# Fused attention and expert layer on one core: a pair's product with v issued behind the third tile of scores instead of the second

## The chip, the cores and the metric

The kernel runs on one core of one Trainium2 chip. The metric is device time in microseconds (us) of one execution; where several runs are compared, their median. PE is TensorE's matmul side and PEld its weight loads, DVE is VectorE, ACT is ScalarE, POOL is GpSimd, and SP is SyncE, which issues the DMAs of this kernel from one queue (SPq).

## The reference, cut to what matters

Two layers follow each other. The first is causal attention with a decay (4 batches, 8 heads, 576 positions, head size 64), the second a sum over 4 experts on the 2304 rows of its result (width 512, inner width 1024):

```python
scores = scale * np.matmul(q, k.transpose(0, 1, 3, 2))
scores = np.where(causal, -1000000000.0, scores + decay)
scores = scores - np.max(scores, axis=-1, keepdims=True)
attn = np.exp(scores)
attn = attn / (np.sum(attn, axis=-1, keepdims=True) + 1e-09)
x = np.matmul(attn, v)            # heads side by side: (2304, 512)
...
for e in range(4):
    h = np.maximum(x @ w1[e], 0.0)
    out += p[:, e:e + 1] * (h @ w2[e])
```

## The kernel before, in words

Attention is cut into 32 jobs. A job is a batch, a pair of heads and a half of the query rows: the first half is rows 0 to 255, the second half rows 256 to 575 against all 576 keys. All first halves come before all second halves (table JOBS, line 43). The change concerns the 16 jobs of the second half, called pairs here; `s1_0_1_1_4_0`, say, is scores of batch 1, head pair 0, half 1, head 1 of the pair, row tile 4, first piece. The first head of a pair is called even here, the second odd.

A head of the second half takes these steps:

- **Preparation.** ACT rounds q and k to a high part (`hi`, line 568), and POOL forms the rest (lines 569, 577, 583).
- **Scores.** For each of three row tiles (2, 3 and 4) `qk_tile` (line 661) has PE form the scores (line 623) in one of four PSUM banks of the pool `ps_a` (tile 4 is cut into two pieces of 288 columns, in two banks). DVE adds the mask and takes the minimum of the negated row (line 637), and ACT takes the exponential with the row sum (line 652).
- **Reciprocal.** DVE forms it from the row sums (`recip16`, lines 680 and 683).
- **Turning.** `turn16` (line 699) splits the scaled probabilities into two float16 parts, `z` high on ACT (line 721) and `z` low on DVE (line 722), in four pieces, and turns them with three DMA transposes on SP's queue (line 731) into a buffer `pt`, of which there are three for all heads.
- **Product.** `av_pair` (line 811) multiplies both heads' `pt` with v in 28 matmuls (line 823) that alternate between the two heads, into a bank of `ps_a`. `out16` (line 874) copies the result with ACT (line 877) into the expert layer's input.

The experts run at the same time on the rows that are finished: steps of a first product (`l1`, line 1019), a gate on ACT and DVE (`gh`, line 1033, and `gl`, line 1034), a second product (`l2`, line 1053) and a sum on DVE (`acc`, line 1080). Their weights are split in three places of ACT, DVE and POOL (lines 980 to 986). PE has both kinds of work in one stream, and the text calls a wait of PE for `gl` or `acc` a wait for the experts' DVE work.

What sets the order around the change: `head_steps(n)` (line 893) writes down the steps of head n as a list with costs: `qs` holds the three score tiles (584, 712 and 776), the reciprocal and the three turns. Into it goes the product of the pair that ended two heads before (cost 1000), with `out16` and the marks `ready`, after which the rows of a chunk count as finished. This is done only where head n is odd, so each pair's product stands among the score tiles of the next pair's odd head. `pace` (line 1566) hands these steps out between the expert steps in proportion to their costs, and a scheduler of the tile framework then orders each engine's instructions by the dependences. After the last pair the list of scores is empty, so the product of the last pair is not moved among tiles. When the attention is done, the inputs of four more chunks are scaled and combined (lines 261, 1170 to 1172), and a second stage of the experts (line 1291) takes over from about 575 us on.

Of the kernel before, what the change touches and what calls it, by code (L numbers as in the profile page):

```python
# [79 lines left out]
def fused(ctx: ExitStack, tc: tile.TileContext, qk, v, f, probs, w, out):  # L80
# [812 lines left out]
    def head_steps(n):  # L893

        st = []
        if FIRST < n < len(heads) and heads[n][1] == 0:
            st.append((0, heads[n][0].prep_v))
        if n + 1 < len(heads):
            j, hh = heads[n + 1]
            st.append((0, lambda j=j, hh=hh: j.prep(hh)))  # L900
        if n + 2 < len(heads):
            j, hh = heads[n + 2]
            st.append((0, lambda j=j, hh=hh: j.far(hh)))
            st.append((0, lambda j=j, hh=hh: j.load(hh)))
        qs, ts, us = [], [], []
        if n < len(heads):
            j, hh = heads[n]
            for t in j.its:
                qs.append((TOK0[t] + 328, lambda j=j, hh=hh, t=t: j.qk_tile(hh, t)))
            if j.half:  # L910
                qs.append((0, lambda j=j, hh=hh: j.recip16(hh)))
                for t in j.its:
                    qs.append((0, lambda j=j, hh=hh, t=t: j.turn16(hh, t)))
            elif hh == 1:
                qs.append((0, j.recip))
        if n - 2 >= FIRST and heads[n - 2][1] == 1 and heads[n - 2][0].half:
            j = heads[n - 2][0]
            qs[2:2] = [(1000, j.av_pair), (0, j.out16)] + ready(n - 2)
        if n - 2 >= FIRST and heads[n - 2][0].half == 0:
            j, hh = heads[n - 2]  # L920
            late_ = [(200, lambda j=j, hh=hh: j.av(hh))]
            if hh == 1:
                late_ += [(0, j.fin)] + ready(n - 2)
            qs[1:1] = late_
        if FIRST < n <= len(heads):
            j, hh = heads[n - 1]
            for gi in range(len(j.blocks())):
                ts.append((500, lambda j=j, hh=hh, gi=gi: j.tr(hh, gi)))
        if n + 1 < len(heads):
            j, hh = heads[n + 1]  # L930
            us.append((0, lambda j=j, hh=hh: j.begin(hh)))
        for k in range(max(len(qs), len(ts))):
            st += ts[k : k + 1] + qs[k : k + 1]
        return st + us
# [577 lines left out]
    def ready(n):  # L1512
        return [(0, c) for c in sorted(done_at) if done_at[c] == n]
# [3 lines left out]
    for n in range(FIRST, len(heads) + 2):  # L1517
        for cost_, f_ in head_steps(n):
            if type(f_) is int:
                if f_ < LAST[0]:  # L1520
                    asteps.extend(turn(f_))
                need[f_] = len(asteps)
            else:
                asteps.append((cost_, f_))
# [103 lines left out]
    j = heads[FIRST][0]  # L1628
# [162 lines left out]
```

## Time and profile before

| | before |
|---|---|
| median of 3 runs | 910.04 us (909.53 to 910.26) |
| the profiled execution | 913.29 us |
| span of its profile | 911.5 us |
| PE busy | 876.0 us (96%) |
| DVE busy | 712.5 us (78%) |
| ACT busy | 568.8 us (62%) |
| POOL busy | 521.7 us (57%) |

The span is what the profile covers of the profiled execution: 1.79 us of its time lie outside. The profiled execution took 3.25 us (0.36%) more than the median of the runs. Times in rows are counted from the start of the span. The second halves of the attention lie between about 208 and 574 us.

### The profile page before, as it was taken

Reading aid. Unit: us, or ns where it says so; the run is one execution under the profiler, and the core shown is the slowest. Engines: PE = TensorE matmul, PEld = TensorE weight load, DVE = VectorE, ACT = ScalarE, POOL = GpSimd, SP = SyncE. Lnnn points to the kernel's source line nnn. Section 1 sums busy time; section 2 is a strip of 40 time slices with the busy share of each in tenths; the row PEclk is TensorE's granted clock in tenths of the full one; section 3 lists DMA queues with packets and bytes.
Section 4 is the critical chain, followed back from the end, with each engine's and each line's share of the span. In section 5 each row is a group of like instructions: output and inputs, shape, how many; then the busy total and the mean of one; then the engine's idle time right before and its main releaser. Section 6 shows DMA issues by size and latency. Waiting matters only on the chain. (4 is left out here: it accounts for less than half of the span.)

```text
span 911.5 us, 16657 instructions
## 1 busy us (share of the span) xinstructions
PE 876.0 (96%) x5783; PEld 617.8 (68%) x5783; DVE 712.5 (78%) x1464; ACT 568.8 (62%) x1137; POOL 521.7 (57%) x522
## 2 busy tenths in 40 slices
PE   3899999999998999999999999989999999999998
PEld 2789898998876666666766666644456654666547
DVE  5768887877999878899888886766688847787487
ACT  5768876657776667677776775645565445553350
POOL 4656556665465454356552772885778627886160
PEclk9999999999999999999999999999999999999999
DMA  7348763665789969979997998834322424232003
GB/s 271 126 151 288 249 232 124 187 195 167 243 203 234 261 175 241 241 211 208 269 289 174 249 244 182 296 126 138 125 79 95 140 70 139 71 112 74 24 1 94
DMA packets 147508, 159.45 MB, mean 175 GB/s; under 512 B 86148, under 2 KB 107328, under 8 KB 147424
## 3 DMA queue, kind: packets, MB, share of 16 engines
q1 hardware_dynamic: 147424, 158.39, 61.1%
q8 instruction: 45, 0.74, 0.3%
q14 instruction: 39, 0.32, 0.1%
HBM read 117.30 MB, written 21.65 MB: 152 GB/s over the span
## 5 line engine op out<-in xcount | busy, mean ns | idle before, releaser
L1019 PE MATMUL l<-y,w 128*128 128x256 f16 x1248 | 154.1, 274 | 0.0
L652 ACT ACTIVATE p<-p,nm 128x576 f32<-128x576 f32 (+3 forms) x160 | 95.7, 599 | 74.2 <-DVE nm L637 61.2
L1019 PEld LDWEIGHTS <-w 128*128 128x128 f16 x1248 | 117.8, 98 | 30.8 <-issue 7.3
L1053 PE MATMUL l<-w,gh 128*128 128x512 f16 x408 | 122.0, 380 | 1.9 <-DVE acc L1080 1.8
L569 POOL CAST q<-raw 64x320 fp32r<-64x320 f32 (+1 forms) x56 | 27.6, 494 | 145.6 <-PE s L623 119.6
L722 DVE SCALAR_TENSOR_TENSOR z<-p,rs,z 128x384 f16<-128x384 f32 (+3 forms) x128 | 82.8, 673 | 13.2 <-ACT z L721 11.9
L1080 DVE SCALAR_TENSOR_TENSOR acc<-y,scg,acc 128x256 f32<-128x256 f32 (+1 forms) x164 | 80.9, 516 | 12.1 <-PE y L1291 11.7
L577 POOL TENSOR_TENSOR kl<-raw,hi 64x576 fp32r<-64x576 f32 (+1 forms) x56 | 68.0, 1214 | 38.7 <-ACT hi L568 36.7
L623 PE MATMUL s<-hi 128*128 128x384 f32 (+1 forms) x192 | 75.8, 399 | 11.4 <-DVE hi L583 8.8
L1291 PE MATMUL m<-rh,bs 128*128 128x512 f16 x256 | 86.4, 379 | 0.0
L637 DVE CUSTOM_DVE_ANT_0 p<-s,mask 128x288 f32<-128x288 f32 (+2 forms) x160 | 74.7, 475 | 13.4 <-PE s L623 12.7
L1217 POOL TENSOR_TENSOR bs<-wt,bs 128x512 f16<-128x512 f32 x32 | 40.5, 1270 | 66.5 <-ACT bs L1216 66.3
L1053 PE MATMUL l<-w,gl 128*128 128x512 f16 x204 | 77.2, 379 | 0.7 <-DVE gl L1034 0.7
L721 ACT ACTIVATE z<-p,rs 128x384 f16<-128x384 f32 (+3 forms) x128 | 69.4, 589 | 5.7 <-DVE rs L683 2.7
L1019 PE MATMUL l<-xh,wh 128*128 128x256 f32 x224 | 65.7, 295 | 1.0 <-ACT xh L864 1.0
L1019 PE MATMUL l<-xh,wl 128*128 128x256 f32 x224 | 64.9, 292 | 1.4 <-POOL wl L962 1.3
L1034 DVE SCALAR_TENSOR_TENSOR gl<-l,gh 128x512 f16<-128x512 f32 (+1 forms) x80 | 54.8, 685 | 14.5 <-ACT gh L1033 13.9
L1291 PE MATMUL m<-rh,bw 128*128 128x512 f16 x191 | 64.4, 379 | 1.4 <-ACT r L1337 1.4
L623 PE MATMUL s<-kl,q 66*128 66x384 f32 (+1 forms) x192 | 62.7, 331 | 3.2 <-DMA kl<-nc 3.2
L1019 PE MATMUL l<-xl,wh 128*128 128x256 f32 x224 | 65.3, 291 | 0.0
L1033 ACT ACTIVATE gh<-l 128x512 f16<-128x512 f32 (+1 forms) x80 | 47.1, 589 | 26.8 <-PE l L1019 26.2
L1291 PEld LDWEIGHTS <-bs 128*128 128x128 f16 x384 | 37.5, 98 | 38.4
(385 smaller groups left out, 2343.9 us busy)
## 6 DMA issues: line engine op xcount, KB each, us to landing
wr<-in_w SPq DMA_DIRECT2D x90, 512.0 KB
pk<-in_w SPq DMA_DIRECT2D x64, 256.0 KB
wd<-w SPq DMA_DIRECT2D x32, 512.0 KB
raw<-in_qk SPq DMA_DIRECT2D x32, 448.0 KB
bw<-wd SPq DMA_DIRECT2D x32, 256.0 KB
bv<-wd SPq DMA_DIRECT2D x32, 256.0 KB
raw<-in_qk SPq DMA_DIRECT2D x24, 256.0 KB
vp<-in_v SPq DMA_DIRECT2D x10, 512.0 KB
```

The lines of the kernel that those rows point to most:

```text
L577: eng.tensor_tensor(out=kl[:64, :wk], in0=r[:64, ko : ko + wk], in1=hi[:64, ko : ko + wk].bitcast(F32), op=ALU.subtract,)
L623: nc.tensor.matmul(out=ps[:, at : at + z - a], lhsT=lhsT, rhs=rhs, start=(m == 0), stop=(m == 1),)
L637: nc.vector.tensor_tensor_reduce(out=pt[:, a:z], in0=ps, in1=mask[:, m0 + a : m0 + z], scale=-0.125, scalar=BIG if n == 0 else nm[:, col : ...
L652: nc.scalar.activation(out=pt[:, :w_], in_=pt[:, :w_], func=AF.Exp, scale=-1.0, bias=self.nmax[hh][:, c : c + 1], accum_out=self.ssum[:, h ...
L721: nc.scalar.activation(out=o[:, 0], in_=x, func=AF.Copy, scale=sc)
L722: nc.vector.scalar_tensor_tensor(out=o[:, 1], in0=x, scalar=sc, in1=o[:, 0], op0=ALU.mult, op1=ALU.subtract)
L1019: i = nc.tensor.matmul(out=self.l1p[:, fi, :], lhsT=lhsT, rhs=rhs[:, k, :], start=(k == 0 and m == 0), stop=(k == 3 and m == 2),)
L1033: self.first = nc.scalar.activation(out=self.gh, in_=self.l1p, func=AF.Relu)
L1034: self.last = nc.vector.scalar_tensor_tensor(out=self.gl, in0=self.l1p, scalar=0.0, in1=self.gh.bitcast(F32) if wide else self.gh, op0=ALU ...
L1053: matmul(out=l2[tt], lhsT=lhsT, rhs=rhs, start=(self.ps == 0 and fi == 0 and m == 0), stop=(self.ps == 1 and fi == 1 and m == 2),)
L1080: nc.vector.scalar_tensor_tensor(out=acc[c][:, tt, d0:d1], in0=ps, scalar=sc, in1=acc[c][:, tt, d0:d1], op0=ALU.mult, op1=ALU.add,)
L1291: line.append(nc.tensor.matmul(**args))
```

## The change

One line of `head_steps`: the product, its copy and the marks are put into the list at index 3, so behind the score tiles 2, 3 and 4 and ahead of the reciprocal and the turns; before, they stood at index 2, between tiles 3 and 4.

```diff
@@ head_steps(n)
         if n - 2 >= FIRST and heads[n - 2][1] == 1 and heads[n - 2][0].half:
             j = heads[n - 2][0]
-            qs[2:2] = [(1000, j.av_pair), (0, j.out16)] + ready(n - 2)
+            qs[3:3] = [(1000, j.av_pair), (0, j.out16)] + ready(n - 2)
```

It acts on 15 of the 16 pairs. Since the costs keep their places but for this one swap, `pace` hands some steps out earlier or later than before, and the scheduler orders the engines anew. Three places show it.

PE, batch 0: the scores of the odd head of pair 2 (`s0_2_1_1`, tiles 2, 3 and 4) and the product of pair 1 (`o0_1_1`), which is due among them, then the first rows of pair 2's own product (`o0_2_1`). Before:

```order
L623 MATMUL s0_2_1_1_2_0_3643<-hi0_2_1_1_3501 128x384
...
L623 MATMUL s0_2_1_1_3_0_3674<-hi0_2_1_1_3501 128x512
...
L823 MATMUL o0_1_1_3700<-pt0_1_1_0_3310,v20_1_1_3207 64x320
...
L623 MATMUL s0_2_1_1_4_0_3756<-hi0_2_1_1_3501 128x288
...
L623 MATMUL s0_2_1_1_4_1_3759<-hi0_2_1_1_3501 128x288
...
L823 MATMUL o0_1_1_3700<-pt0_1_1_1_3480,v20_1_1_3207 64x320
...
L823 MATMUL o0_2_1_3999<-pt0_2_1_0_3602,v20_2_1_3498 64x320
...
L823 MATMUL o0_2_1_3999<-pt0_2_1_1_3767,v20_2_1_3498 64x320
```

With the change:

```order
L623 MATMUL s0_2_1_1_2_0_3627<-hi0_2_1_1_3481 128x384
...
L623 MATMUL s0_2_1_1_3_0_3654<-hi0_2_1_1_3481 128x512
...
L623 MATMUL s0_2_1_1_4_0_3682<-hi0_2_1_1_3481 128x288
...
L623 MATMUL s0_2_1_1_4_1_3685<-hi0_2_1_1_3481 128x288
...
L823 MATMUL o0_1_1_3715<-pt0_1_1_0_3299,v20_1_1_3194 64x320
...
L823 MATMUL o0_1_1_3715<-pt0_1_1_1_3460,v20_1_1_3194 64x320
...
L823 MATMUL o0_2_1_4008<-pt0_2_1_0_3588,v20_2_1_3478 64x320
...
L823 MATMUL o0_2_1_4008<-pt0_2_1_1_3748,v20_2_1_3478 64x320
```

Between this head's last scores and the first row of its own pair's product stand 254 rows of PE's order before and 326 with the change. For the pairs from 3 to 14 it is about 200 before and about 350 with the change; for the last pair 68 and 148.

DVE, the same head: from its last minimum (`p0_2_1_1_4`) to the low parts of its probabilities (`z1`, `z3`). Before (the rows left out are the second weight split, two sums, four minima of the next head, the preparation of v and rows on scales):

```order
L637 ISA p0_2_1_1_4_3616,nm0_2_1_1_3617<-s0_2_1_1_4_1_3759,mask_115,nm0_2_1_1_3617 128x288
L637 ISA nm0_2_1_1_3617 128x1
L1034 SCALAR_TENSOR_TENSOR gl1_0_2_0_3750<-l1_1_0_2_0_3693,gh1_0_2_0_3749 128x512
L285 TENSOR_REDUCE wmax_121<-pk1_14_3634 128x1
L986 SCALAR_TENSOR_TENSOR w36_3815<-wr36_3253,wsc_122,w36_3815 128x512
...
L680 TENSOR_SCALAR ss0_2_1_3496<-ss0_2_1_3496 128x3
...
L683 RECIPROCAL rs0_2_1_3497<-ss0_2_1_3496 128x3
...
L1034 SCALAR_TENSOR_TENSOR gl1_0_2_1_3865<-l1_1_0_2_1_3834,gh1_0_2_1_3864 128x512
...
L722 SCALAR_TENSOR_TENSOR z1_3003<-p0_2_1_1_2_3614,rs0_2_1_3497,z1_3003 128x3x128
```

With the change:

```order
L637 ISA p0_2_1_1_4_3602,nm0_2_1_1_3603<-s0_2_1_1_4_1_3685,mask_115,nm0_2_1_1_3603 128x288
L637 ISA nm0_2_1_1_3603 128x1
L680 TENSOR_SCALAR ss0_2_1_3476<-ss0_2_1_3476 128x3
L683 RECIPROCAL rs0_2_1_3477<-ss0_2_1_3476 128x3
L722 SCALAR_TENSOR_TENSOR z1_2973<-p0_2_1_1_2_3600,rs0_2_1_3477,z1_2973 128x3x128
L722 SCALAR_TENSOR_TENSOR z1_2973<-p0_2_1_1_3_3601,rs0_2_1_3477,z1_2973 128x4x128
L722 SCALAR_TENSOR_TENSOR z3_2975<-p0_2_1_1_4_3602,rs0_2_1_3477,z3_2975 64x4x128
L722 SCALAR_TENSOR_TENSOR z3_2975<-p0_2_1_1_4_3602,rs0_2_1_3477,z3_2975 64x64
L637 ISA p0_3_1_0_2_3760,nm0_3_1_0_3763<-s0_3_1_0_2_0_3799,mask_115 128x384
```

The odd head's low parts now stand right behind its own minima, where two gate subtractions, two weight splits, two sums, four minima and the preparation of v stood between them before.

POOL, the preparation of the even head of pair 1 and the low parts of two expert weights (`wl30`, `wl31`). Before:

```order
L962 TENSOR_TENSOR wl30_2962<-wr30_2374,wh30_2961 128x512 x2
L962 TENSOR_TENSOR wl31_2969<-wr31_2583,wh31_2968 128x512 x2
...
L569 CAST q2_0_116<-raw0_1_1_0_2867 64x320
L577 TENSOR_TENSOR kl0_1_1_0_2865<-raw0_1_1_0_2867,hi0_1_1_0_3022 64x576
L583 TENSOR_TENSOR hi0_1_1_0_3022<-raw0_1_1_0_2867,hi0_1_1_0_3022 64x320
```

With the change:

```order
L569 CAST q2_0_116<-raw0_1_1_0_2860 64x320
L577 TENSOR_TENSOR kl0_1_1_0_2858<-raw0_1_1_0_2860,hi0_1_1_0_2992 64x576
L583 TENSOR_TENSOR hi0_1_1_0_2992<-raw0_1_1_0_2860,hi0_1_1_0_2992 64x320
L962 TENSOR_TENSOR wl30_3002<-wr30_2374,wh30_3001 128x512 x2
L962 TENSOR_TENSOR wl31_3009<-wr31_2583,wh31_3008 128x512 x2
```

The preparation has moved ahead of the two weights' low parts. On SP's queue the transposes of the odd heads have moved ahead of weight loads and stores in the same way (those of pair 6, for one, now stand ahead of the load `wr46` and of the stores `wd10` and `wd11`).

## Rows read from the trace of the kernel before

**Rows 1.** The page, part 1: busy time of each engine over the whole span.

```profile
PE 876.0 (96%) x5783; PEld 617.8 (68%) x5783; DVE 712.5 (78%) x1464; ACT 568.8 (62%) x1137; POOL 521.7 (57%) x522
```

**Rows 2.** Waits of PE, 240 to 640 us: total us, times, longest us.

```profile
PE o L823 <- DMA pt<-z: 5.5, 4, 2.2
PE l L1053 <- DVE acc L1080: 1.8, 3, 1.3
PE l L1053 <- DVE gl L1034: 0.7, 1, 0.7
```

**Rows 3.** Groups of PE, 240 to 640 us: busy, mean ns, idle before and its releaser.

```profile
L823 PE MATMUL o<-pt,v 128*64 128x320 f16 (+2 forms) x448 | 31.2, 281 | 5.6 <-DMA pt<-z 5.5
```

**Rows 4.** Timeline, odd head and product of pair 2: start, duration, work, [idle before, releaser].

```profile
266.57 0.30 PE L623 MATMUL s<-kl,q 66*128 66x288 f32 x1
...
280.27 2.99 DVE L722 SCALAR_TENSOR_TENSOR z<-p,rs,z 128x384 f16<-128x384 f32 x2 [0.25 <-ACT z L721]
282.01 4.25 SPq L731 DMA_TRANSPOSE pt<-z  x3
...
285.24 0.32 PE L823 MATMUL o<-pt,v 128*64 128x320 f16 x1
...
288.07 1.69 PE L823 MATMUL o<-pt,v 128*64 128x320 f16 x27 [2.19 <-DMA pt<-z]
```

**Rows 5.** Timeline, the last pair: its last transpose and its product.

```profile
567.93 1.23 SPq L731 DMA_TRANSPOSE pt<-z  x1
...
571.91 1.72 PE L823 MATMUL o<-pt,v 128*64 128x320 f16 x27
```

**Rows 6.** Windows: busy us of PE, PEld, DVE, ACT, POOL, granted clock, DMA share.

```profile
240.00:270.00 30.00, 29.59 (x222) 22.97 (x222) 27.97 (x57) 23.18 (x47) 14.21 (x14) 1.00 0.79 192
270.00:300.00 30.00, 27.69 (x199) 19.01 (x198) 28.53 (x59) 22.22 (x46) 18.34 (x14) 1.00 1.03 245
300.00:330.00 30.00, 27.79 (x192) 18.92 (x190) 23.30 (x59) 17.57 (x35) 9.42 (x14) 0.94 0.93 244
450.00:480.00 30.00, 29.32 (x207) 19.51 (x205) 25.96 (x57) 22.47 (x45) 15.37 (x15) 1.00 1.08 275
```

**Rows 7.** Timeline, product of pair 3 and expert matmuls; one from before pair 2's product.

```profile
283.83 1.47 PE L1019 MATMUL l<-y,w 128*128 128x256 f16 x12
...
310.56 2.74 PE L823 MATMUL o<-pt,v 128*64 128x320 f16 x27 [2.21 <-DMA pt<-z]
313.24 2.05 PE L1019 MATMUL l<-y,w 128*128 128x256 f16 x12
```

**Rows 8.** Window of one us behind that wait.

```profile
312.00:313.00 1.00, 1.00 (x14) 0.96 (x11) 0.71 (x2) 0.00 (x0) 0.00 (x0) 0.50 0.96 344
```

**Rows 9.** Groups of DVE by shape, 260 to 570 us.

```profile
L722 DVE SCALAR_TENSOR_TENSOR z<-p,rs,z 64x512 f16<-64x512 f32 x29 | 23.6, 814 | 0.9
L722 DVE SCALAR_TENSOR_TENSOR z<-p,rs,z 128x512 f16<-128x512 f32 x29 | 22.3, 770 | 0.0
L722 DVE SCALAR_TENSOR_TENSOR z<-p,rs,z 128x384 f16<-128x384 f32 x28 | 19.6, 701 | 11.3 <-ACT z L721 11.2
L637 DVE CUSTOM_DVE_ANT_0 p<-s,mask 128x512 f32<-128x512 f32 x27 | 18.4, 680 | 0.1
L637 DVE CUSTOM_DVE_ANT_0 p<-s,mask 128x384 f32<-128x384 f32 x27 | 14.8, 546 | 1.0 <-PE s L623 0.8
L722 DVE SCALAR_TENSOR_TENSOR z<-p,rs,z 64x64 f16<-64x64 f32 x29 | 12.5, 430 | 0.1
```

**Rows 10.** Groups of ACT by shape, 220 to 560 us.

```profile
L652 ACT ACTIVATE p<-p,nm 128x576 f32<-128x576 f32 x30 | 23.2, 773 | 29.0 <-DVE nm L637 28.8
L721 ACT ACTIVATE z<-p,rs 128x384 f16<-128x384 f32 x31 | 18.8, 606 | 4.1 <-DVE rs L683 2.7 <-ACT p L652 0.8 <-ACT gh L1033 0.2
```

**Rows 11.** Waits, whole span: POOL's preparation of heads.

```profile
POOL q L569 <- PE s L623: 126.9, 35, 12.5
```

**Rows 12.** Transposes into pt, whole span: min/median/max ns, first and last.

```profile
L731 SPq DMA_TRANSPOSE pt<-z x96: 1198/1258/4662, 221.6 to 567.9; - x96
```

## The prediction

> **What bounds the kernel.** I read the page's busy times first: PE is busy for 876.0 us of the span and DVE for 712.5 [rows 1], so time is won where PE stands idle, or loses its clock, and nothing on another engine counts unless PE waits for it. Then the waits of PE over the second halves of the attention: the largest entry is the product with v waiting for the transposed probabilities, 5.5 us in four waits, the longest 2.2 [rows 2]. The same stretch's group of line 823 has 5.6 us idle over 448 matmuls, that is 16 pairs of 28 [rows 3]. The 0.1 between them is a fifth, very short wait.
>
> Where do these waits come from? In the timeline of pair 2 the odd head's last scores end at 266.87 (266.57 and 0.30). DVE turns to the low parts of its probabilities only at 280.27, 13.4 us later, the three transposes are issued from 282.01 to 286.26, and PE, which had begun the product at 285.24, waits 2.19 us until 288.07 [rows 4]. The last transpose thus needs 1.8 us from the end of its issue until PE goes on. So a pair waits when its odd head's transposes are issued too late, and most of the lateness is not work of that head. It is DVE doing other things between its minima and its low parts. Pair 3 has the same shape with 2.21 us [rows 7].
>
> Its price is more than the gap. [...] PE's work shows it, since the same 27 matmuls take 2.74 us there and 1.69 at pair 2, and twelve expert matmuls 2.05 instead of 1.47 [rows 4, 7].
>
> **The change, part by part.** The product and the third tile change places, so the product itself costs the same. What counts is the distance from the odd head's last scores to its own product.
>
> *The waits for transposes: -5.6 us.* Before, the product of the pair ahead sat in the middle of the odd head and held its third tile back. Now the tile goes first, and 326 rows of PE's order stand where 254 stood at pair 2, some 350 where 200 stood at the pairs behind it. Every second row is a weight load, which runs beside the matmuls, so 70 more rows are 35 matmuls or, at the 1.47 us of twelve [rows 7], 4.3 us more cover, and 150 rows 9.2. The longest wait is 2.21, so both ends of that are enough. On DVE the low parts now stand right behind the head's own minima, which takes several more us off. I take all five waits as gone: 5.6. The ends are 5.6 and, if SP's queue held the transposes back, 0 (rival B).
>
> *The clock: -0.9 us.* Of two nearly equal waits, 2.19 and 2.21, one was followed by the lower clock and one was not [rows 4, 7, 8]. [...] If new waits arise, the clock may fall behind one of these. Ends -1.8 and 0, the middle taken. [...]
>
> *New waits for DVE: +2.0 us.* DVE's total work is the same, but it comes earlier. In 270 to 300 us DVE is busy for 28.53 us, so 1.47 are free, while PE's time in it shrinks by pair 2's 2.19 us [rows 4, 6]: DVE is 0.7 short. Besides, from the gate subtraction of expert step 0_7_0_1, in which the second halves begin, to that of step 1_1_2_0, counting rows in both orders, DVE has nine heads' low parts now against eight, and one minimum of tile 2 and one of tile 3 fewer. A head's low parts are 0.70 + 0.77 + 0.81 + 0.43 = 2.72 us, the two minima 0.55 + 0.68 [rows 9], so 1.5 us more. Together 2.2; I take 2.0, since some of it falls into 300 to 330 us where DVE has 6.7 us free [rows 6]. It should appear as PE waiting for `gl` or `acc`, as it does now for 0.7 and 1.8 us [rows 2]. Ends: 0, if DVE's overlap between instructions hides it, and 5, if two odd heads also hold DVE up as in rival A.
>
> *POOL and SP: 0.* The preparation of heads mostly waits for the scores of an earlier head to free a buffer (126.9 us in 35 waits [rows 11]), so scores that come earlier are not held by it. Two weights' low parts (`wl30`, `wl31`) have fallen behind one preparation, once in the kernel; their cover is the rest of the expert step, and what is lost if it is missing is bounded by that preparation, under the lower end of the DVE term. On SP's queue weight loads now stand behind transposes. An issue takes 1.26 us at the median and 4.66 at most [rows 12], so a load can be up to 14 us later; a load is issued well ahead of its use and three buffers hold loads, so I put it at nothing, and at 2 us for the high end (a wait like the longest above).
>
> *The last pair and the hand-over: 0.* The last pair is not moved, but the steps around it are. Its last transpose is issued by 569.16 and its product runs from 571.91 without a wait, a distance of 2.75 us against the 1.8 it needs [rows 4, 5], so 1 us of reserve. The order has 148 rows instead of 68 between its scores and its product, so the reserve is not smaller. Behind it the inputs of the next chunks are scaled, and PE waits there for `acc`, 1.3 us at the longest [rows 2]. It can close or double: ends -1.3 and +1.3, taken as 0.
>
> Sum: -5.6 - 0.9 + 2.0 = -4.5 us. The profiled execution took 913.29 us, 3.25 above the median of the runs, so 908.8 against it, and **905.5** against the median of 910.04. I assume that the median's runs have the same waits.
>
> **Rivals.**
>
> *A, slower: DVE stands still behind the odd head's own exponential.* The low parts right behind the last minimum have to wait for ACT: the exponential of tile 4 at 0.77 us and the first high part at 0.61 [rows 10], 1.4 us in which DVE, which takes its instructions in order, does nothing. Before, other rows filled this. DVE already idles 11.2 us for high parts over 28 heads [rows 9]. In the five pairs up to 330 us, with DVE at 27.97 and 28.53 of 30 [rows 6], nothing absorbs it: 5 x 1.4 = 7.0, with the 2.0 above 9.0, against 5.6 saved, and the clock lost again at new waits, so +3.4 and 913.4. It decides when DVE's free time in 240 to 300 us (3.5 us now) is less than what the heads there leave idle. For it: the order, which puts nothing between. Against it: DVE need not keep up at once, since a gate subtraction may be some us late before PE wants it (PE waited for `gl` once from 240 to 640 us [rows 2]).
>
> *B, no change: the wait only moves.* Either the transposes land when the DMA engines let them (their share is 1.03 to 1.08 of the windows with waits and transposes reach 4.66 us [rows 6, 12]), or DVE gives back the 5.6 us whole, about 910.0. For it: DVE is nearly full just where the waits are. Against: 450 to 480 us has the highest share, 1.08, and PE was still busy for 29.32 of 30.
>
> *C, half: given back at the hand-over.* All before 574 us happens as forecast, but the experts' rest waits for weights or for the scaled inputs as the attention ends earlier: half of the gain, 907.8. For it: the `acc` wait of 1.3 us shows that PE has little reserve there.
>
> That the change would not do what it says, as `pace` could hand the steps out so that nothing moves, the orders exclude.
>
> **How the numbers follow.** A measurement of this kernel can tell about 0.2%, 1.8 us, from no change. The forecast gets 0.56, C 0.16, B 0.13, A 0.15. The forecast's own ends are 910.04 - 5.6 - 1.8 - 1.3 = 901.3 and 910.04 - 5.6 + 5 + 2 = 911.4, of which most lies below 908.2. Faster: 0.53 of the forecast and 0.12 of C, 0.65. Same: the rest of both (0.07) and B, 0.20. Slower: A, 0.15. The range goes from 901.8 to 911.4, which leaves out the larger part of A and little else; without A and B it would be 902 to 908.5.
>
> **What would show it.** Right: no idle time, or under 0.5 us, at line 823, and over 5 us from the end of an odd head's transposes to its product; a granted clock of 1.00 over 300 to 330 us; new waits of PE for `gl` or `acc` before 330 us that sum to 1 to 4 us. Rival A shows as DVE idle for ACT at lines 680 and 722 in 210 to 330 us with PE waiting for `gl` for over 5 us; B as waits at line 823 of the same size; C as more than 2 us of PE idle in 574 to 620 us. The forecast is wrong if line 823 still waits for over 2 us in sum, or if the PE waits for DVE before 330 us exceed the saved 5.6.

## The result and the profile after

With the change the kernel took **919.04 us** (median of 4 runs, 917.20 to 920.33), against 909.78 (908.41 to 910.26) for the kernel before in the same comparison: a ratio of 1.0095, interval 1.008 to 1.011. It is slower by about 9 us. I had forecast 905.5 with a range of 901.8 to 911.4, so both the sign and the range were wrong. The profiled execution of the changed kernel took 920.33 us (span 918.6).

The page's busy times answer to [rows 1]:

```profile
PE 876.5 (95%) x5783; PEld 615.4 (67%) x5783; DVE 714.6 (78%) x1464; ACT 568.8 (62%) x1137; POOL 523.6 (57%) x522
```

PE is as busy as before, 876.5 us against 876.0, so the time has gone into idle PE. These are the four largest waits of PE from 240 to 640 us (total us, times, longest us), against [rows 2]:

```profile
PE l L1053 <- DVE acc L1080: 4.0, 3, 2.4
PE o L823 <- DMA pt<-z: 3.0, 2, 2.4
PE m L1291 <- ACT r L1337: 2.5, 1, 2.5
PE topx L200 <- DVE xmax L261: 1.1, 1, 1.1
```

The product with v, which waited 5.5 us in four waits, still waits 3.0, and that in two. The long one of the two is in a new place, the last pair. `topx` (PE turning a maximum that DVE has formed) is new in this stretch, and so are, further down the list, two waits for weights (`w`, 0.8 us each); the wait for `r` (the second stage's copy on ACT) has grown from 0.6 us.

The windows (busy us of PE, PEld, DVE, ACT, POOL, granted clock, DMA share) show where; the first two answer to [rows 6]:

```profile
270.00:300.00 30.00, 30.00 (x216) 20.58 (x216) 26.81 (x57) 23.08 (x48) 18.08 (x15) 1.00 1.04 235
300.00:330.00 30.00, 27.90 (x206) 19.06 (x204) 25.88 (x67) 18.37 (x38) 12.51 (x14) 1.00 0.89 230
...
540.00:570.00 30.00, 27.57 (x207) 18.43 (x205) 19.82 (x42) 15.13 (x33) 10.17 (x7) 0.95 0.69 167
570.00:600.00 30.00, 27.79 (x177) 16.88 (x176) 22.50 (x34) 15.88 (x27) 20.34 (x20) 1.00 0.71 246
600.00:630.00 30.00, 25.07 (x120) 12.06 (x119) 14.55 (x20) 12.66 (x21) 15.90 (x18) 0.94 0.48 158
```

The first two went nearly as forecast: no idle PE from 270 to 300 us, and a clock of 1.00 from 300 to 330 instead of 0.94, with 2.1 us of new waits for DVE. The loss is in the last three, where PE is idle for 2.43, 2.21 and 4.93 us and the clock is below full twice (0.95 and 0.94). The same three windows of the kernel before had PE busy for 30.00, 29.61 and 27.78 us at 1.00. So the change loses its time behind 560 us, at the last pair and the hand-over to the next chunks.

PE's timeline there (start, duration, work, idle before and its releaser):

```profile
551.04 0.30 PE L623 MATMUL s<-kl,q 66*128 66x288 f32 x1
...
559.90 0.32 PE L823 MATMUL o<-pt,v 128*64 128x320 f16 x1
...
562.11 1.69 PE L1019 MATMUL l<-y,w 128*128 128x256 f16 x14
566.23 2.67 PE L823 MATMUL o<-pt,v 128*64 128x320 f16 x27 [2.43 <-DMA pt<-z]
568.83 1.92 PE L1019 MATMUL l<-y,w 128*128 128x256 f16 x10
...
585.11 0.39 PE L1019 MATMUL l<-y,w 128*128 128x256 f16 x2 [0.82 <-ACT w L985]
586.28 2.58 PE L1019 MATMUL l<-y,w 128*128 128x256 f16 x22 [0.78 <-DVE w L986]
...
605.19 0.59 PE L1053 MATMUL l<-w,gh 128*128 128x512 f16 x2 [2.43 <-DVE acc L1080]
...
614.53 0.56 PE L1291 MATMUL m<-rh,bs 128*128 128x512 f16 x1 [2.49 <-ACT r L1337]
```

The first row is the last of the scores of the last odd head. Before, the last product ran without a wait [rows 5]. Now it waits 2.43 us for its transposes, and it stands in the middle of one group of 24 gate matmuls of the experts: 14 of them ahead of it, 10 behind. Four more waits follow, of 0.82, 0.78, 2.43 and 2.49 us. With three short ones between 595 and 599 us (0.14, 0.22, 0.24) this is 9.55 us of idle PE; before, the stretch had 0.29, 1.30, 0.44 and 0.59, so 2.62.

The other queues in that stretch show what links the waits (same columns; ACT, SP's queue, DVE and POOL in order of time):

```profile
552.91 3.19 DVE L986 SCALAR_TENSOR_TENSOR w<-wr,wsc,w 128x512 f16<-128x512 f32 x2
...
558.55 2.21 ACT L721 ACTIVATE z<-p,rs 128x384 f16<-128x384 f32 x4 [0.49 <-ACT p L652]
...
559.88 4.29 SPq L731 DMA_TRANSPOSE pt<-z  x3
...
568.94 0.68 ACT L877 ACTIVATE xf<-o,vun 128x64 f32<-128x64 f32 x2 [6.99 <-PE o L823]
568.99 1.27 POOL L1170 TENSOR_TENSOR rx<-xf,xf 128x512 f32<-128x512 f32 x1 [4.92 <-PE o L823]
569.28 2.35 DVE L261 TENSOR_REDUCE xmax<-xf 128x1 f32<-128x1024 f32 x2 [6.44 <-ACT xf L877]
...
570.79 0.60 ACT L1033 ACTIVATE gh<-l 128x512 f16<-128x512 f32 x1 [1.18 <-PE l L1019]
571.29 0.71 ACT L985 ACTIVATE w<-wr,wsc 128x512 f16<-128x512 f32 x1
...
575.50 0.33 SPq L943 DMA_DIRECT2D wr<-in_w  x1
...
581.98 0.72 ACT L985 ACTIVATE w<-wr,wsc 128x512 f16<-128x512 f32 x1 [5.38 <-DMA wr<-in_w]
```

The transposes are issued until 564.17 and the product goes on at 566.23, 2.06 us later, near the 1.8 us of [rows 4]. But behind the product stand ACT for 6.99 us, POOL for 4.92 and DVE for 6.44: each has the product's output, or what is made from it, at the head of its queue, and the weights of the next expert steps behind that. ACT splits the next weight at 571.29, its buffers come free late (SP's queue waits 8.7 us for DVE's split of a weight and 0.6 for POOL's), the next load is issued at 575.50, and ACT can split that weight at 581.98, for which PE then waits at 585.11. So the delay is carried on through four queues.

Before, ACT and PE had another order there (the odd head's last scores end at 560.31):

```profile
563.00 2.21 ACT L721 ACTIVATE z<-p,rs 128x384 f16<-128x384 f32 x4 [0.50 <-ACT p L652]
...
569.17 0.72 ACT L985 ACTIVATE w<-wr,wsc 128x512 f16<-128x512 f32 x1
...
570.94 1.04 PE L1019 MATMUL l<-y,w 128*128 128x256 f16 x8
...
573.56 1.92 PE L1019 MATMUL l<-y,w 128*128 128x256 f16 x16
573.66 0.68 ACT L877 ACTIVATE xf<-o,vun 128x64 f32<-128x64 f32 x2 [2.12 <-PE o L823]
```

There the high parts start 2.7 us behind the last scores, with the change 7.2 (558.55 against 551.34). ACT splits the next weight 4.5 us ahead of the product's copy, with the change 2.35 us behind it. The product stood in the middle of a gate group before as well (8 matmuls ahead of it, 16 behind), without a wait and without loss.

### The profile page after: what moved, and what is told of

It reads as the page before. It is cut to its first block, busy times and chain, and to the rows that moved or that the text cites. A ratio compares the mean times of both kernels' runs of the same rounds, so it can differ in the third digit from the quotient of the medians.

```text
span 918.6 us, 16640 instructions
## 1 busy us (share of the span) xinstructions
PE 876.5 (95%) x5783; PEld 615.4 (67%) x5783; DVE 714.6 (78%) x1464; ACT 568.8 (62%) x1137; POOL 523.6 (57%) x522
## 5 line engine op out<-in xcount | busy, mean ns | idle before, releaser
L577 POOL TENSOR_TENSOR kl<-raw,hi 64x576 fp32r<-64x576 f32 (+1 forms) x56 | 65.5, 1169 | 56.5 <-ACT hi L568 55.6
L569 POOL CAST q<-raw 64x320 fp32r<-64x320 f32 (+1 forms) x56 | 30.1, 538 | 94.5 <-PE s L623 88.4
L981 POOL TENSOR_TENSOR w<-wr,w 128x512 f16<-128x512 f32 x32 | 43.1, 1355 | 37.7 <-ACT w L980 37.6
```

The costliest lines, as they stand in the source:

```text
L577: eng.tensor_tensor(out=kl[:64, :wk], in0=r[:64, ko : ko + wk], in1=hi[:64, ko : ko + wk].bitcast(F32), op=ALU.subtract,)
```

## The experiments

In the list of head n, the product that moves is that of the odd head n - 2: n = 35 is pair 0, n = 49 pair 7, n = 63 pair 14. All edits are to the changed kernel. The place of pair 14's product (n = 63) is in the odd head of the last pair, 15, and is called the last place.

| run | product behind the third tile in | median us | before | ratio, interval |
|---|---|---|---|---|
| the change | pairs 0 to 14 | 919.04 | 909.78 | 1.0095, 1.008 to 1.011 |
| e1_not_last | pairs 0 to 13 | 910.97 | 910.39 | 0.9999, 0.9985 to 1.0014 |
| e2_only_last | pair 14 | 918.63 | 910.39 | 1.0087, 1.0057 to 1.0116 |
| e3_first_half | pairs 0 to 6 | 906.62 | 910.39 | 0.9962, 0.9946 to 0.9979 |
| e4_second_half | pairs 7 to 14 | 924.20 | 910.39 | 1.0151, 1.0123 to 1.0180 |
| e6_pairs_1_6 | pairs 1 to 6 | 907.98 | 910.23 | 0.9978, 0.9963 to 0.9993 |
| e10_pairs_0_3 | pairs 0 to 3 | 909.74 | 910.26 | 1.0002, 0.9988 to 1.0017 |
| e5_last_later | pairs 0 to 14, filler | 924.90 | 910.23 | 1.0167, 1.0152 to 1.0182 |
| e7_out_dve | pairs 0 to 14, last copy on DVE | 917.66 | 910.23 | 1.0097, 1.0072 to 1.0123 |
| e8_split_pool | pairs 0 to 14, two half splits on POOL | 918.90 | 910.23 | 1.0104, 1.0088 to 1.0121 |
| e9_hold | pairs 0 to 14, last product later | 910.73 | 910.26 | 1.0004, 0.9993 to 1.0015 |

### Which places lose the time

```diff
-            qs[3:3] = [(1000, j.av_pair), (0, j.out16)] + ready(n - 2)
+            i = 3 if n < 63 else 2      # e1_not_last
+            i = 3 if n == 63 else 2     # e2_only_last
+            i = 3 if n < 49 else 2      # e3_first_half
+            i = 2 if n < 49 else 3      # e4_second_half
+            qs[i:i] = [(1000, j.av_pair), (0, j.out16)] + ready(n - 2)
```

(One of the four lines with `i` in each kernel.) Expected of e1_not_last:

> The change at 14 of its 15 places; the product of pair 14, which stands in the list of the last pair's odd head, stays at index 2. Theory T (tail): up to 560 us the change gains 4 to 5 us, and all of the loss comes from the last place, which brings the last pair's scores and product too close together: here 904 to 907 us, the last pair's product without a wait. Rival G (given back): whatever runs ahead in the attention is lost at the hand-over, however its end is ordered: 909 to 919 us, with PE waiting after 565 us for over 6 us. Rival S (spread): each of the 15 places costs about 0.6 us: 917 to 919 us.

Expected of e2_only_last:

> The change at its last place only. Theory T: no gain before 540 us and the loss behind it: 917 to 921 us, a wait of 2 us or more at the last pair's product and the lower clock behind it. Rival G: nothing runs ahead, so nothing is given back: 909 to 911 us. Rival S: 910 to 911 us.

Expected of e3_first_half:

> The change at the 7 places of pairs 0 to 6 only (both batches that come first, less one pair). Theory T: the waits at line 823 of pairs 1, 2 and 3 are gone and the end is ordered as in the kernel before: 904 to 907 us. Rival G: the lead of some 4 us is lost behind 565 us: 909 to 914 us. Rival S: about 914 us.

Expected of e4_second_half:

> The change at the 8 places of pairs 7 to 14 only. Theory T: the three long waits at line 823 before 315 us stay, at most 1 us of waits behind 420 us goes, and the end is lost as in the changed kernel: 915 to 920 us. Rival G: no lead, no loss: 909 to 911 us. Rival S: about 914 us.

The last place alone costs as much as the whole change: 8.2 us with nothing else moved (918.63 less 910.39), and 8.1 as the difference between the change and e1_not_last (919.04 less 910.97). The first seven pairs gain 3.8 us, and pairs 7 to 13 lose again what they gain: 4.4 us from e3_first_half to e1_not_last, 5.6 from e2_only_last to e4_second_half. The three parts, -3.8, +4.4 and +8.1, lead from one kernel to the next, so they add to the whole by themselves: +8.7 against the 910.39 of that comparison, +9.3 against the 909.78 of the first.

e2_only_last and e3_first_half came out as theory T said, though e2's wait is 1.93 us and not 2. The other two missed. e1_not_last is over T's 904 to 907, and in rival G's range without G's waits of over 6 us behind 565 us (2.9 here). e4_second_half is 4 us over T's range and far from both rivals, so pairs 7 to 13 cost what no theory had in it. Rival S fits none of the four.

In e2_only_last the order of PE's and DVE's instructions is that of the kernel before up to the last pair, and the late waits are those of the changed kernel, a little different in size. Its last product waits 1.93 us and is followed by waits of 1.11 and 0.78 us for weights, 1.85 for `acc` and 2.48 for `r`. In e1_not_last this product waits 0.28 us and in e3_first_half not at all.

For pairs 7 to 13 the window from 450 to 560 us tells part of it. First e3_first_half, in which those pairs are as before (columns as above):

```profile
450.00:560.00 110.00, 109.84 (x820) 75.58 (x818) 93.66 (x209) 78.98 (x163) 59.02 (x49) 1.00 0.86 227
```

and e1_not_last, in which they are moved:

```profile
450.00:560.00 110.00, 107.88 (x805) 74.10 (x804) 93.03 (x201) 78.67 (x161) 56.48 (x48) 1.00 0.82 217
```

PE loses 1.96 us in it, and PE's timeline of e1_not_last has the three waits that make it up:

```profile
454.71 0.59 PE L1054 MATMUL l<-w,gh 128*128 128x512 f16 x2 [0.88 <-DVE acc L1081]
...
466.81 0.39 PE L1054 MATMUL l<-w,gl 128*128 128x512 f16 x1 [0.42 <-DVE gl L1035]
...
521.08 0.59 PE L1054 MATMUL l<-w,gh 128*128 128x512 f16 x2 [0.76 <-DVE acc L1081]
```

The first of them is in the changed kernel too, and DVE's timeline there shows its cause (one PE row, from PE's timeline, at the end):

```profile
448.88 0.74 DVE L1080 SCALAR_TENSOR_TENSOR acc<-l,scg,acc 128x512 f32<-128x512 f32 x1
...
450.64 1.36 DVE L722 SCALAR_TENSOR_TENSOR z<-p,rs,z 128x384 f16<-128x384 f32 x2 [0.73 <-ACT z L721]
451.92 0.75 DVE L1080 SCALAR_TENSOR_TENSOR acc<-l,scg,acc 128x512 f32<-128x512 f32 x1
...
452.72 0.59 PE L1053 MATMUL l<-w,gh 128*128 128x512 f16 x2 [0.89 <-DVE acc L1080]
```

Between the two sums that free PE's accumulator stand the odd head's low parts, and ahead of them DVE waits 0.73 us for ACT's high part. That is what rival A describes, at one place. The other 2.4 us of the 4.4 that pairs 7 to 13 lose I could not place. In e4_second_half, where these pairs lose 5.6 us, most of it shows: PE waits there 5.9 us for `acc` and 1.1 for `gl` from 405 to 535 us, where e2_only_last waits 1.0 us at line 823, and its idle PE from 190 to 564 us is 10.2 us against 5.6.

Two smaller cuts of the same kind:

```diff
+            i = 3 if 35 < n < 49 else 2    # e6_pairs_1_6
+            i = 3 if n < 43 else 2         # e10_pairs_0_3
```

> The change at the 6 places of pairs 1 to 6; at pair 0's the product stays at index 2. The run with pairs 0 to 6 gave 906.6 us. Theory B: at the place of pair 0 the four tiles of scores in a row make PE wait for PSUM banks that DVE's minima free, 1.3 us at 223 to 228 us; here these waits are gone and the waits at line 823 stay away: 904 to 906 us. Rival: the place of pair 0 is also what makes pair 1's transposes come in time; without it a wait at line 823 of 1 to 2 us is back: 907 to 909 us.

> The change at the 4 places of pairs 0 to 3 only, whose own products (pairs 0 to 3) and whose odd heads (pairs 1 to 4) cover the three longest waits at line 823. If the gain of the run with pairs 0 to 6 (906.6 us) comes from these waits alone: 904 to 907 us, with no wait over 0.7 us at line 823 before 320 us. If the places behind them add to it by running ahead: 907 to 910 us.

e6_pairs_1_6 gains 2.2 us, e10_pairs_0_3 nothing, although its profile has no wait at line 823 before 330 us and 0.2 us in all. So the gain doesn't follow from the product's waits alone: in e10_pairs_0_3 PE waits 1.53 us for `acc` at 399 us, behind the last moved pair, where e3_first_half has no wait. What makes that wait was not tried. In e6_pairs_1_6 I had looked for the scores' waits for the minima at 224 to 228 us to go with pair 0's place. They stayed (1.2 us), so pair 0's place is not their cause. The rival's 907 to 909 us holds 907.98, but not its wait of 1 to 2 us at line 823 (0.5), so neither theory is borne out.

### What makes the last place dear

Four edits were to tell whether the late transposes or a busy ACT or DVE is behind the 8 us. The first three missed.

```diff
+            if n == 65:                          # e5_last_later
+                qs.append((1500, lambda: None))
```

> The changed kernel with an empty step of cost 1500 in the list between the last pair's scores and its product, so that PE has 228 rows between them where the changed kernel has 196. Theory W: the last product's wait of 2.4 us starts the loss at the end (the lower clock behind it, ACT held in its queue, weights split late, PE waiting for them and for acc): without the wait 910 to 914 us, and less than 3 us of PE idle from 560 to 615 us. Rival H: the hand-over loses on its own, since the last pair's scores and the experts' last steps stand in another order: 916 to 919 us, with the waits behind 580 us still there.

The empty step was to give the last head more expert work ahead of its product. But its cost enters the pace of all steps: 924.90 us, with waits of 2.5 us for `acc` at 404 and 3.1 for `rh` at 592 that no other kernel here has. The last product still waited 1.04 us, here between whole gate groups. It tells nothing of the question.

```diff
+                if self is jobs[-1]:             # e7_out_dve
+                    nc.vector.tensor_scalar(
+                        out=self.x_of(c)[:, self.pr, o : o + n], in0=self.op[0][:, d : d + n],
+                        scalar1=vun, scalar2=None, op0=ALU.mult,
+                    )
+                    continue
```

> The changed kernel with the last pair's copy of the product on DVE instead of ACT, so that ACT isn't held for 7 us behind the late product. Theory A: the weights are then split in time, PE's waits of 1.6 us for them at 584 to 587 us go, and what follows shrinks by as much: 914 to 917.5 us. Rival: the weights are late for their loads on SP's queue or for POOL, not for ACT: 918 to 920 us with these waits as they are.

With the last copy on DVE, ACT no longer stands behind the product itself, and yet 917.66 us and the waits for weights (1.19 and 1.12) stay. ACT's timeline of this kernel shows why:

```profile
570.12 0.60 ACT L1039 ACTIVATE gh<-l 128x512 f16<-128x512 f32 x1 [7.13 <-PE l L1025]
570.61 0.71 ACT L991 ACTIVATE w<-wr,wsc 128x512 f16<-128x512 f32 x1
```

ACT now waits 7.13 us for the gate group, whose last 10 matmuls PE has behind the product, and the weight split at 570.61 is 3.4 us behind the product's restart (567.17), with the change 5.1. That gain of 1.6 us is all clock (1.00 from 555 to 570 us, with the change 0.89): the 27 and 10 matmuls behind the wait took 1.72 and 1.26 us in this profile, instead of 2.67 and 1.92. It is PE's order that holds ACT, whichever instruction stands first. And the lower clock right behind the wait is not what costs most, since this execution took 917.83 us without it.

```diff
-                if k == 1:                       # e8_split_pool
+                if k == 1 or n in (58, 59):
```

> The changed kernel with the first halves of two expert weights (58 and 59) split by POOL instead of DVE. In the changed kernel these two splits, 3.2 us of DVE, stand between the minima of tiles 3 and 4 of the last pair's odd head, and nothing else in the orders differs. Theory W: the minima come 3 us earlier, the last product's wait of 2.4 us goes, and with it most of the loss at the end: 910 to 914 us. Rival H: the wait goes and the time stays within 2 us of the changed kernel: 917 to 920 us.

This took two half splits of weights (the 3.19 us at 552.91 above) off DVE ahead of the last head's minima. The last minimum ended 2.7 us behind the head's last scores instead of 5.8. But ahead of the sums that the low parts need, DVE has a gate subtraction, and waited 0.89 us for its `gh`, and line 680 took 1.07 us instead of 0.17. So z started 5.7 us behind the scores instead of 7.2, and of that the three transposes, issued in 5.55 us instead of 4.29, used up most. The product still waits 2.10 us, the time stays at 918.90. That is rival H's range, but H wanted the wait gone, so neither is tested.

```diff
         while m < len(asteps) and cost[m + 1] <= goal:
             m += 1
+        if n < 74.75:                            # e9_hold
+            m = min(m, 635)
         upto(m)
```

> The changed kernel with nothing moved but the last pair's product and what follows it: they are held back by 10 matmuls of line 1019 and 9 of line 1053, 3.1 us of PE at the rows' pace, DVE's order being the same. Theory W: the wait of 2.4 us at this product and the lower clock behind it go, but what depends on the product comes at most 0.7 us later than now; the later waits for weights, acc and r go with it as far as the wait caused them: 911 to 915 us. Rival H: the later waits (1.6 us for weights, 2.4 for acc, 2.5 for ACT's r) come from the order of the experts' last steps against the second stage's preparation and stay: 916 to 919 us with no wait at line 823.

This one is the same kernel up to the last pair's product, with the same order of DVE up to its low parts. From its second matmul on, the product stands 19 matmuls, about 3.1 us, later on PE: the 10 gate matmuls that were behind it are now ahead, with 9 of line 1053. Time 910.73 us, ratio 1.0004: 8.3 us less than the change, for moving 3.1 us of work from behind a wait to in front of it. That is 0.3 us below theory W's range and far from rival H's. Its timeline (PE, ACT and SP's queue):

```profile
563.46 2.78 PE L1019 MATMUL l<-y,w 128*128 128x256 f16 x24
...
566.28 0.60 ACT L1033 ACTIVATE gh<-l 128x512 f16<-128x512 f32 x1 [3.04 <-PE l L1019]
566.78 0.71 ACT L985 ACTIVATE w<-wr,wsc 128x512 f16<-128x512 f32 x1
...
568.12 1.80 PE L823 MATMUL o<-pt,v 128*64 128x320 f16 x28
...
569.96 0.68 ACT L877 ACTIVATE xf<-o,vun 128x64 f32<-128x64 f32 x2 [0.82 <-PE o L823]
...
570.96 0.33 SPq L943 DMA_DIRECT2D wr<-in_w  x1
...
577.06 0.72 ACT L985 ACTIVATE w<-wr,wsc 128x512 f16<-128x512 f32 x1 [3.13 <-DMA wr<-in_w]
```

The gate group is whole (x24), ACT makes `gh` at 566.28 instead of 570.79, splits the weight at 566.78 instead of 571.29, and the load goes out 4.5 us earlier, at 570.96. The product runs as 28 matmuls in one piece. The waits behind it shrink to 0.50, 0.61, 0.36, 0.44 and 0.58 us, though the product's output comes hardly earlier: 17.3 us behind the odd head's last scores, which end at 552.64 here, against 17.6 in the changed kernel. So what costs is not when the product ends, but what stands behind it.

Three things go with this edit: the wait is gone, the gate group is whole, and ACT and DVE have the weight splits ahead of the product's copy and its maximum instead of behind. The split group alone does not cost, as the kernel before has it. The wait and the order of the queues were not parted. The kernels with the order of the change there tell a little: e4_second_half waits only 1.66 us at this product, at the full clock behind it (27 matmuls in 1.72 us, 1.00 from 570 to 600 us), and its later waits are 1.23, 0.78, 2.44 and 2.48 us, not shorter than the change's 0.82, 0.78, 2.43 and 2.49. So that the order would lose by itself, without a wait, is not excluded.

## Why the prediction was wrong, point by point

**The last pair and the hand-over: 0.** This is the step that failed. I wrote that its order has "148 rows instead of 68 between its scores and its product, so the reserve is not smaller", with ends of -1.3 and +1.3. It measured +8.1 us. Four things were wrong in it. I counted rows to the product's first matmul, but PE waits at the second: to that one the order has 196 rows with the change and 164 before, nearly the same. I looked at PE alone: DVE has two weight splits of 3.19 us together between this head's scores and its last minimum, so z starts 7.2 us behind the last scores where it was 2.7, and the transposes land 2.43 us too late. The reserve of 1 us rested on the 1.8 us of pair 2 alone. For pair 3 of the same trace the issues end at 307.10 and PE goes on at 310.56 [rows 7], 3.46 us later, by which the 2.75 us of the last pair are no reserve:

```profile
301.08 6.02 SPq L731 DMA_TRANSPOSE pt<-z  x3
```

And I priced what can go wrong there at 1.3 us, a wait at about its own length. Here PE stands at a point behind which ACT, DVE, POOL and with them the weight loads are queued, and the place cost 8 us with a wait of 2.43. How much of it is the wait and how much the order of these queues stays open. The upper end of 911.4 even left out this term's own +1.3; with it, 912.7, it would still have missed.

**The waits for transposes: -5.6.** Up to 564 us this went nearly as forecast: of 5.6 us, 0.6 are left, at pair 1 (266.89), and pairs 2 to 14 have 8 us and more from their last transpose to their product. But the saving is not quite the same in each execution. In e2_only_last, with the order of before there, pair 3 waited 0.56 us instead of 2.21 and the places ahead of the last pair 5.1 in sum; in e4_second_half, which has that order up to pair 6, its first seven pairs waited 2.5 us instead of 4.8. My sum rested on one execution that was 3.25 us above the median, and I had only assumed that the others have its waits.

**The clock: -0.9.** No run shows this term itself, the middle of two ends; the 1.8 us of its full end are my estimate from the trace of before, 0.06 of the 30 us from 300 to 330, where the clock was 0.94 [rows 6]. What the runs showed in its place: the dip went away, 300 to 330 us is at 1.00, so 1.8 us. The order of before has one such dip (0.94) in each of the three profiles that have it, once at 300 to 330 and twice at 270 to 300 us. But new dips came behind the new waits, 0.95 from 540 to 570 and 0.94 from 600 to 630, or 1.5 and 1.8 us lost.

**New waits for DVE: +2.0.** Mis-sized. Up to 564 us the changed kernel has new waits for the minima (0.25, 0.55, 0.40, 0.15), `topx` (1.06), `acc` (1.04, 0.89, 0.64) and `gl` (0.42): 5.4 us, against 1.1 before (0.69 for `gl`, 0.24 for `acc`, 0.15 for `topx`), so +4.3. Only part of it has the form that I named, `gl` or `acc`: the minima and `topx` I had not thought of. My count of DVE's surplus stopped at 330 us, where 3.45 of the 5.4 are. The rest are in pairs 7 to 13, for which I had put nothing, and which lose 4.4 us where they had little to gain (0.68 us at line 823, at 469 us). All idle PE from 190 to 564 us is 6.8 us before, 6.0 with the change, 5.9 in e1_not_last and 4.7 in e3_first_half. So the first seven pairs have a gain to show, and behind them hardly any is left.

**POOL and SP: 0.** No wait of PE is put down to POOL before 560 us, and none to a weight load on SP's queue. POOL's preparation waits less for scores, 95.3 us in 33 waits, than in [rows 11].

**Rivals.** A said that DVE stands still behind the odd head's exponential. DVE's waits for it grew a little (whole span, us, times, longest):

```profile
DVE ss L680 <- ACT p L652: 13.8, 18, 0.9
DVE z L722 <- ACT z L721: 10.8, 16, 1.3
```

The first was 9.2 in 14 before, the second 11.9 in 16, so 3.5 us more in all, and `acc` shows it at 452 us. From 210 to 330 us, for which A had 7.0, the two are 2.8 and 2.9 against 1.0 and 2.9, so 1.8 more. e3_first_half, the fastest, has as much of both (14.2 and 11.3), so this standing alone does not make a kernel slower. A's time, 913.4, came out nearer than my own by luck. B, that the wait moves, is right in kind, but it moved to the last pair, where I had counted on a reserve. C named the place, the hand-over, but with half of a gain given back, not a loss of twice the gain.

**The signs I had named.** Line 823 waits for 3.0 us in sum, over the 2 from which I called the forecast wrong. Idle PE from 574 to 620 us is 7.1 us, where I had put the sign of rival C at over 2. The waits for DVE before 330 us, 3.45 us, stayed under the 5.6 of the other sign.

Best of all kernels run is e3_first_half, which moves the product in pairs 0 to 6 alone: 906.62 us against 910.39, ratio 0.9962 (0.9946 to 0.9979), faster than both the kernel before and the changed one. There a gain of the forecast's size exists, 3.8 us of 4.5, though by e10_pairs_0_3 the waits at line 823 alone do not explain it.

## What to carry to other kernels

Before moving a wait to the end of a stage, read what stands behind it in the queues of the other engines: where other engines have that result at the head of their queues and the next stage's inputs behind it, the place can cost several times the wait, as here 8 us with 2.4. Count the distance to the instruction that waits, not to the first of its group, and look at the order of every engine on the way to it. A change that repeats over many places is best tried in parts, since here seven places gained, seven lost, and one cost more than all others together.

## What the runs showed of the hardware

A gap of some 2.2 us doesn't always cost the clock. In the kernel before, 2.19 us at pair 2 did not (1.00 from 270 to 300 us) and 2.21 at pair 3 did (0.50 from 312 to 313 us) [rows 4, 6, 7, 8]. In e2_only_last and e4_second_half, in PE's order the same there, it was pair 2's: 2.25 and 2.22 us, followed by 27 matmuls in 3.17 and 2.76 us instead of 1.69, and 0.94 from 270 to 300 us. At the last pair 2.43 us did in the changed kernel (27 matmuls in 2.67 us, 0.89 from 555 to 570 us) and 2.33 in e7_out_dve did not (1.72, at 1.00).

At the hand-over, instructions of DVE and POOL took longer beside each other. DVE's timeline of the changed kernel:

```profile
588.07 4.17 DVE L1172 SCALAR_TENSOR_TENSOR rl<-xf,xsc,rh 128x512 f16<-128x512 f32 x3
592.16 1.40 DVE L1172 SCALAR_TENSOR_TENSOR rl<-rx,xsc,rh 128x512 f16<-128x512 f32 x2
```

and POOL's:

```profile
584.53 1.15 POOL L1217 TENSOR_TENSOR bs<-wt,bs 128x512 f16<-128x512 f32 x1 [0.85 <-ACT bs L1216]
...
588.52 1.60 POOL L1217 TENSOR_TENSOR bs<-wt,bs 128x512 f16<-128x512 f32 x1
...
592.98 1.71 POOL L1170 TENSOR_TENSOR rx<-xf,rx 128x512 f32<-128x512 f32 x1 [1.29 <-DVE rl L1172]
```

From 592.16 to 592.98, with POOL idle, DVE takes 0.70 us for one; beside POOL's instructions 1.39 in the mean, and POOL's `bs` takes 1.60 instead of 1.15. No run here shows why. The kernel before has such long instructions too (its eight `rl<-rx` of line 1172 take 1.24 us in the median, 0.74 at the least); how much of the 8 us comes from it was not tried.
